# PSUM pools that take over banks wait for single tiles; transposes spread three steps apart: a routed attention with a feed-forward on one core

## Chip, core and metric

The kernel runs on one core of a Trainium2 chip. The metric is the device time of one execution in microseconds (us), lower is better. A core has five engines with queues of their own: TensorE (PE, with its weight loads as PEld), VectorE (DVE), ScalarE (ACT), GpSimd (POOL) and SyncE (SP), which issues transfers. Each executes its instructions in program order and waits at semaphores for the others.

## What is computed

Attention for 4 batches of 8 heads, 768 positions, head size 64. A query sees only those keys that are nearest to the same one of 16 centroids of its head. The result goes through a normalization and a gated feed-forward from 512 to 1536 and back.

```python
q_assign = np.argmax(np.einsum('bhsd,hcd->bhsc', q_n, c_n), axis=-1)
k_assign = np.argmax(np.einsum('bhsd,hcd->bhsc', k_n, c_n), axis=-1)
mask = q_assign[:, :, :, None] == k_assign[:, :, None, :]
scores = scale * np.matmul(q, k.transpose(0, 1, 3, 2))
scores = np.where(mask, scores, -1000000000.0)
scores = scores - np.max(scores, axis=-1, keepdims=True)
attn = np.exp(scores)
attn = attn / (np.sum(attn, axis=-1, keepdims=True) + 1e-09)
out = np.matmul(attn, v)
# ... heads side by side: x is [3072, 512]
rms = np.sqrt(np.mean(x * x, axis=-1, keepdims=True) + 1e-06)
xn = x / rms * rms_g
g = xn @ w_gate
silu = g * (1.0 / (1.0 + np.exp(-g)))
val = xn @ w_val
return silu * val @ w_out
```

## The kernel before

Work goes by pairs of heads (16 pairs `pi`) and by steps: 9 score chunks for each of the 32 heads ("slots"). Pair `pi` has its scores in steps `18 pi` to `18 pi + 17`. The main loop issues a step's scores, a piece of the feed-forward, the product with the values for the head before, and then whatever was put at that step with `at(step, fn)`. The order of the calls is the order of the instructions on each engine.

The preparation of a pair has thirteen parts. Four transposes on PE (T0 to T3, tile `tp`), each copied to SBUF; the casts into `aug` on GpSimd (CAST); the centroid products (SP, tile `sp`); then on VectorE a chain that makes the one-hot rows: transpose to `tr`, maximum `mx`, comparison `oh`, its scaling, transpose back to `ohT` (TR, MX, CMP, SCL, BACK); four transfers of `ohT` into `aug` (PLACE); and the cast of the values (CASTV).

```python
        def t_group(g):
            # ...
                tp = t_tile("tp")              # one bank of ps_t in the main loop
            for i in range(TH):
                nc.tensor.transpose(tp[:, i * P:(i + 1) * P], src[:, a, i * P:(i + 1) * P], ident_f)
            # ...
            if on_dve:
                nc.vector.tensor_copy(dst, tp)
            else:
                nc.scalar.copy(dst, tp)
```

Up to step 95 (`FFN0 = 96`) a score tile `scw` is three banks wide and serves three steps; there are two of them. From step 96 on the same six banks are given to `sc` (two), `gv` (two), `d` and `t` (one each), and the feed-forward runs beside the attention.

```python
    def score_chunk(slot, j):
        # ...
        if slot * NCH + j < FFN0:
            if j % WCH:
                return
            nch = WCH                          # 3
            sc = late["wide"].tile([P, WCH * CH], F32, name="scw", tag="scw")
        else:
            sc = late["sc"].tile([P, CH], F32, name="sc", tag="sc")
        # ... matmuls of aug with aug
        nc.scalar.activation(pts[slot][:, j * CH:(j + nch) * CH], sc[:, :nch * CH], ACT.Exp, scale=scale)
```

The product with the values goes into `acc`, of which there is one tile (`ps_pv`, `bufs=1`): six groups, in chunks 2 to 7 of the next head; in chunk 8 `pv_norm` divides it into `x`, after which the next head may use it.

```python
    def pv_norm(slot):
        # ...
        nc.vector.reciprocal(inv, acc[:, :, D:D + 1])
        nc.vector.tensor_tensor(x_t[b][:, :, h * D:(h + 1) * D], acc[:, :, 0:D],
                                inv.to_broadcast([P, ST, D]), op=ALU.mult)
```

At the end of a batch `x` is squared and summed by position block (`sumsq`, tiles `jk` and `ss`; for batch 0 first the columns of six heads, then those of the last two), raised to -1/2 on GpSimd (`ir`), scaled to `xn` and turned by PE (`turn`, tile `tx`) or by a transfer into `xnT`, the operand of the feed-forward (`gp`, `vp`, `dp`).

```python
    first.close()
    late["wide"] = wide.enter_context(tc.tile_pool(name="ps_wide", bufs=2, space=PSUM))
    # ...
    for step in range(NT):
        slot, j = divmod(step, NCH)
        if step == FFN0:
            wide.close()
            for nm, bufs in (("sc", 2), ("gv", 2), ("d", 1), ("t", 1)):
                late[nm] = ctx.enter_context(tc.tile_pool(name="ps_" + nm + "2", bufs=bufs, space=PSUM))
        score_chunk(slot, j)
        ffn_next(min(B, max(0, (step - LAG) // (H * NCH))) * 2 * FC, on_act=False)
        flush(1)
        if slot > 0 and 2 <= j < 2 + ST:
            pv_group(slot - 1, j - 2)
        if slot > 0 and j == 2 + ST:
            pv_norm(slot - 1)
        extras(step)
```

Of the kernel before, what the change touches and what calls it, by code (L numbers as in the profile page):

```python
# [13 lines left out]
PSUM = bass.MemoryType.PSUM  # L14
# [5 lines left out]
def kernel(  # L20
# [12 lines left out]
    nc = tc.nc  # L33
    B, H, S, D = q.shape
    NC = centroids.shape[1]
    DM, DF = moe_w_gate.shape
# [31 lines left out]
    wide = ExitStack()  # L68
    WCH = 3
    late = {}  # L70
# [16 lines left out]
    def load_pair(pi, kinds=range(3)):  # L87
        for kind in kinds:
            load_part(pi, kind)
# [7 lines left out]
    g_b = const.tile([P, DM], F32, name="g_b")  # L97
# [64 lines left out]
    def w_load(i):  # L162
        if i < 8:
            j, kind = divmod(i, 2)
            c = slice(j * DF // 4, (j + 1) * DF // 4)
            nc.gpsimd.dma_start(out=(wg, wv)[kind][:, :, c],
                                in_=(moe_w_gate, moe_w_val)[kind][:, c].rearrange("(c p) f -> p c f", p=P))
        else:
            j = i - 8
            nc.gpsimd.dma_start(  # L170
                out=wo[:, 3 * j:3 * j + 3, :],
                in_=moe_w_out[j * 3 * P:(j + 1) * 3 * P, :].rearrange("(c p) d -> p c d", p=P))
# [114 lines left out]
    def score_chunk(slot, j):  # L287
        pi, a = divmod(slot, 2)
        ag = aug[pi % NSET][a]
        if j == 0:  # L290
            pts[slot] = ptp.tile([P, ST * S], BF16, name="pT", tag="pT")
        nch = 1
# [3 lines that stand above are left out]
            nch = WCH  # L296
# [3 lines that stand above are left out]
        lo = j * CH  # L300
        while lo < (j + nch) * CH:
            kc, qo = divmod(lo, S)
            o = lo - j * CH
            n = min(CH - o % CH, S - qo)
            nc.tensor.matmul(sc[:, o:o + n], lhsT=ag[:, 1, kc * P:(kc + 1) * P],  # L305
                             rhs=ag[:, 0, qo:qo + n], start=True, stop=True)
            lo += n
        nc.scalar.activation(pts[slot][:, j * CH:(j + nch) * CH], sc[:, :nch * CH], ACT.Exp, scale=scale)  # L308
# [3 lines left out]
    def pv_group(slot, g):  # L312
        pi, a = divmod(slot, 2)
        vb = vbf[pi % NSET]
        if g == 0:
            accs[slot] = ps_pv.tile([P, ST, D + 1], F32, name="acc", tag="acc")
        acc = accs[slot]
        for kc in range(ST):
            nc.tensor.matmul(acc[:, TORD[g], :], lhsT=pts[slot][:, kc * S + g * P:kc * S + (g + 1) * P],  # L319
                             rhs=vb[:, a, TORD[kc], :], start=(kc == 0), stop=(kc == ST - 1))  # L320

    def pv_norm(slot):
        b, h = divmod(slot, H)
        if h == 0:
            x_t[b] = xp.tile([P, ST, DM], BF16, name="x", tag="x")
        acc = accs.pop(slot)
        inv = small.tile([P, ST, 1], F32, name="inv", tag="inv")
# [3 lines that stand above are left out]
# [121 lines left out]
    def flush(keep=0):  # L452
        while len(pend) > keep:
            pend.pop(0)()
# [4 lines left out]
    def ffn_next(limit, tail=False, on_act=True):  # L459
        n, kind = divmod(fpos[0], 3)  # L460
        if n >= limit:
            return False
        fpos[0] += 1
        ffn_piece(n, kind, tail, on_act)
        return True
# [6 lines left out]
    def at(step, fn):  # L472
        extra.setdefault(step, []).append(fn)

    T0, T1, T2, T3, CAST, SP, TR, MX, CMP, SCL, BACK, PLACE, CASTV = range(13)
# [22 lines left out]
    p1[CAST]()  # L498
    keep_warm(9, w_ps)
    first.close()  # L500
    late["wide"] = wide.enter_context(tc.tile_pool(name="ps_wide", bufs=2, space=PSUM))
    for i, step in ((SP, 0), (TR, 1), (MX, 1), (CMP, 2), (SCL, 2), (BACK, 3), (PLACE, 3), (CASTV, 3)):
        at(step, p1[i])
    at(3, lambda: load_part(2, 2))
    at(5, lambda: load_part(3, 2))
    at(8, lambda: load_pair(4))
    for i, step in ((CAST, 4), (SP, 6), (TR, 7), (MX, 9), (CMP, 10), (SCL, 10), (BACK, 12), (PLACE, 12), (CASTV, 13)):
        at(step, p2[i])
    at(22, lambda: load_pair(5))
    at(30, lambda: nc.sync.dma_start(out=g_b, in_=moe_rms_g.unsqueeze(0).to_broadcast([P, DM])))  # L510

    at(49, lambda: nc.gpsimd.tensor_scalar_mul(g_b, g_b, DM ** 0.5))
    for b in range(B):
        sumsq, inv, norm, turn = rms_parts(b)
        if b == 0:
            plan = [(sumsq, (-9, 0, 2), (0, 1, 2), 0), (sumsq, (8, 8, 8), (0, 1, 2), 1), (inv, (8,), (0,), 2),
                    (norm, (12, 17, 18), (0, 1, 2)), (turn, (17, 20, 22), (0, 1, 2)),
                    (sumsq, (27, 29, 30), (3, 4, 5)), (inv, (30,), (1,)), (norm, (32, 33, 34), (3, 4, 5))]
        else:
            plan = [(sumsq, (9, 9, 10), (0, 1, 2)), (inv, (11,), (0,)), (norm, (12, 13, 15), (0, 1, 2)),  # L520
                    (sumsq, (19, 19, 25), (3, 4, 5)), (inv, (26,), (1,)), (norm, (27, 28, 29), (3, 4, 5))]
        for fn, steps, items, *more in plan:
            for step, it in zip(steps, items):
                at(H * NCH * (b + 1) + step, lambda fn=fn, it=it, more=more: fn(it, *more))
    for pi in range(3, B * NP):
        base = 2 * NCH * (pi - 2) + {7: 17, 8: 6}.get(pi, 0)
        steps = (-8, -6, -4, -2, 0, 1, 3, 4, 5, 6, 7, 8, 10)
        if pi == 3:
            steps = (-9, -7, -5, -3, 0, 1, 3, 4, 5, 6, 7, 8, 10)
        elif pi == 6:  # L530
            steps = (-8, -6, -4, -2, 0, 1, 3, 4, 5, 5, 6, 7, 21)
        elif pi > 6:
            steps = (-5, -4, -3, -2, 0, 1, 2, 3, 4, 5, 6, 6, 10)
        for fn, step in zip(prep_parts(pi), steps):
            at(base + step, fn)
        if pi < B * NP - 3:
            at({6: 100, 7: 118}.get(pi, base + 12), lambda pi=pi: load_pair(pi + 3))
    for i, step in enumerate((44, 50, 57, 65, 72, 78, 95, 100, 105, 111, 117, 123)):
        at(step, lambda i=i: w_load(i))
    def extras(step):  # L540
        for fn in extra.get(step, ()):
            fn()

    for step in range(NT):
        slot, j = divmod(step, NCH)
        if step == FFN0:
            wide.close()
            for nm, bufs in (("sc", 2), ("gv", 2), ("d", 1), ("t", 1)):
                late[nm] = ctx.enter_context(tc.tile_pool(name="ps_" + nm + "2", bufs=bufs, space=PSUM))
        score_chunk(slot, j)  # L550
        ffn_next(min(B, max(0, (step - LAG) // (H * NCH))) * 2 * FC, on_act=False)
        flush(1)
# [5 lines that stand above are left out]
# [41 lines left out]
```

## Time and profile before

| what | value |
|---|---|
| time, median of 3 | 354.16 us (353.92 to 356.08) |
| span of the profiled execution | 352.4 us |
| mean granted clock of TensorE | 0.995 of full |
| busy: PE, ACT, DVE, POOL | 337.2, 226.6, 223.9, 89.0 us |
| transferred | 34.98 MB, mean 99 GB/s |

The page gives each engine's busy time, the costliest groups of instructions and the chain of work that ended last. In a line of waits "A <- B: total, times, longest" says how long engine and instruction A stood idle until B released it. A line of the timeline has start, length, engine, source line, operation, output and inputs, shapes and count; in brackets the idle time before it and its releaser. Matmuls are pipelined and their ends are modelled, so the distance between starts says more than the length. A granted clock below 1.00 makes each matmul longer without showing idle time.

### The profile page before, as it was taken

What the parts mean: (1) busy time and instruction counts of PE and PEld (TensorE: products, weight loads), DVE (VectorE), ACT (ScalarE), POOL (GpSimd) and SP (SyncE); (2) the same over time, 40 slices, a digit from 0 to 9 for tenths busy, and PEclk for the clock granted to TensorE, in tenths of its full rate; (3) what the DMA queues carried; (4) which work ended last, traced back from release to release, by engine and by line L of the source; (5) the groups of instructions that cost most, each with busy time, mean ns of one, the idle gap of its engine ahead of it and who ended that gap; (6) DMA issues with size and microseconds to landing.
All of it is one profiled execution on the core that took longest, in us unless ns stands there. A gap on an engine that the chain in (4) does not pass through costs nothing.

```text
span 352.4 us, 7515 instructions
## 1 busy us (share of the span) xinstructions
PE 337.2 (96%) x2960; PEld 205.1 (58%) x2960; DVE 223.9 (64%) x460; ACT 226.6 (64%) x389; POOL 89.0 (25%) x123
## 2 busy tenths in 40 slices
PE   8988998899999999999999999999999998999996
PEld 3556665566656566665656566556666654555543
DVE  4786678588774678757566567765554686655540
ACT  3688888787767687766667677777777253323322
POOL 2676854256520324211030304020000011000000
PEclk9999999899999999999999999999999999999999
DMA  7766999947784007161411002220000021300012
GB/s 233 231 210 197 214 250 232 225 59 109 160 222 148 30 15 207 43 168 42 129 50 42 32 12 56 55 53 32 30 8 27 30 56 52 76 30 30 32 60 89
DMA packets 36770, 34.98 MB, mean 99 GB/s; under 512 B 13520, under 2 KB 33664, under 8 KB 36736
## 3 DMA queue, kind: packets, MB, share of 16 engines
q1 hardware_dynamic: 30240, 29.20, 26.6%
q0 software_dynamic: 5984, 4.84, 9.8%
q10 hardware_dynamic: 512, 0.48, 0.5%
q8 instruction: 23, 0.38, 0.4%
q14 instruction: 11, 0.09, 0.1%
HBM read 28.61 MB, written 6.29 MB: 99 GB/s over the span
## 4 chain that ended last, share of the span: by engine, by line
PE 81%; DVE 10%; ACT 3%; DMA 2%; issue 2%; POOL 1%; SPq 0%; DVEq 0%; ACTq 0%; POOLq 0%
PE dp L440 17%; PE gp L407 17%; PE vp L407 16%; PE sc L305 11%; PE acc L319 8%; PE tp L201 5%; PE scw L305 4%; PE sp L237 3%; DVE xn L373 2%; DVE qk L205 2%; DMA k_in<-in_k_dram 1%; ACT pT L308 1%; DVE oh L254 1%; DVE gvT L422 1%; DVE x L329 1%
## 5 line engine op out<-in xcount | busy, mean ns | idle before, releaser
L308 ACT ACTIVATE pT<-sc 128x512 bf16<-128x512 f32 x192 | 113.4, 597 | 47.4 <-PE sc L305 46.4
L416 DVE SCALAR_TENSOR_TENSOR uu<-th,gp 128x384 f32<-128x384 f32 x96 | 53.0, 552 | 62.1 <-ACT th L412 62.0
L407 PE MATMUL vp<-xnT,wv 128*128 128x384 bf16 x384 | 78.1, 325 | 1.8 <-DVE gvT L422 1.8
L407 PE MATMUL gp<-xnT,wg 128*128 128x384 bf16 x384 | 78.1, 325 | 0.5 <-DVE gvT L422 0.5
L440 PE MATMUL dp<-wo,gvT 128*128 128x512 bf16 (+1 forms) x300 | 76.1, 370 | 1.9 <-ACT ob L446 1.9
L412 ACT ACTIVATE th<-gp 128x384 f32<-128x384 f32 x96 | 47.2, 492 | 46.3 <-PE gp L407 43.3
L319 PEld LDWEIGHTS <-pT 128*128 128x128 bf16 x1152 | 57.9, 98 | 29.5 <-issue 3.9
L305 PE MATMUL sc<-aug 80*128 80x512 bf16 (+1 forms) x256 | 72.6, 326 | 1.2 <-ACT pT L308 1.2
L224 POOL CAST aug<-qk 64x768 bf16<-64x768 f32 x60 | 51.7, 862 | 57.5 <-DVE qk L205 50.0
L319 PE MATMUL acc<-vbf,pT 128*128 128x65 bf16 x1152 | 63.4, 194 | 2.1 <-DVE x L329 2.1
L407 PEld LDWEIGHTS <-wg 128*128 128x128 bf16 x384 | 37.1, 97 | 31.9 <-issue 1.3
L422 DVE TENSOR_TENSOR gvT<-uu,vp 128x384 bf16<-128x384 f32 x96 | 52.4, 546 | 4.9 <-PE vp L407 0.4
L308 ACT ACTIVATE pT<-scw 128x1536 bf16<-128x1536 f32 x32 | 44.9, 1452 | 10.3 <-PE scw L305 10.2
L407 PEld LDWEIGHTS <-wv 128*128 128x128 bf16 x384 | 37.0, 97 | 21.0 <-issue 2.7
L305 PEld LDWEIGHTS <-aug 80*128 80x128 bf16 x384 | 33.9, 98 | 19.5 <-issue 8.8
L440 PEld LDWEIGHTS <-gvT 128*128 128x128 bf16 x300 | 29.1, 98 | 26.9 <-issue 2.9
L205 DVE COPY qk<-tp 128x384 f32<-128x384 f32 x40 | 21.9, 554 | 25.9 <-PE tp L201 25.6
L305 PE MATMUL scw<-aug 80*128 80x512 bf16 (+1 forms) x128 | 27.0, 334 | 0.9 <-issue 0.7
L364 POOL TENSOR_SCALAR ir<-ss 128x3 f32<-128x3 f32 x7 | 1.7, 236 | 95.1 <-ACT jk L350 84.7
L373 DVE SCALAR_TENSOR_TENSOR xn<-x,ir,g_b 128x512 bf16<-128x512 bf16 x24 | 20.6, 871 | 6.9 <-POOL ir L365 5.8
L229 POOL CAST vbf<-v_in 128x768 bf16<-128x768 f32 x16 | 13.5, 845 | 38.5 <-issue 38.2
L329 DVE TENSOR_TENSOR x<-acc,inv 128x384 bf16<-128x384 f32 x32 | 17.8, 557 | 1.1
(62 smaller groups left out, 212.2 us busy)
## 6 DMA issues: line engine op xcount, KB each, us to landing
q_in<-in_q_dram SPq DMA_DIRECT2D x16, 384.0 KB, 5.3
k_in<-in_k_dram SPq DMA_DIRECT2D x16, 384.0 KB, 6.0
out_dram<-ob SPq DMA_DIRECT2D x23, 256.0 KB, 2.0
v_in<-in_v_dram SPq DMA_DIRECT2D x15, 384.0 KB, 6.2
wg<-in_moe_w_gate_dram POOLq DMA_DIRECT2D x4, 384.0 KB, 6.3
wv<-in_moe_w_val_dram POOLq DMA_DIRECT2D x4, 384.0 KB, 7.4
wo<-in_moe_w_out_dram POOLq DMA_DIRECT2D x4, 384.0 KB, 6.2
aug<-ohT SPq DMA_DIRECT2D x57, 24.0 KB, 1.9
```

What stands on the lines that cost most here:

```text
L205: nc.vector.tensor_copy(dst, tp)
L224: nc.gpsimd.tensor_copy(aug[st][a][0:D, :, par * HS:(par + 1) * HS], qk32[0][par * D:(par + 1) * D, 2 * a:2 * a + 2, :])
L305: nc.tensor.matmul(sc[:, o:o + n], lhsT=ag[:, 1, kc * P:(kc + 1) * P], rhs=ag[:, 0, qo:qo + n], start=True, stop=True)
L308: nc.scalar.activation(pts[slot][:, j * CH:(j + nch) * CH], sc[:, :nch * CH], ACT.Exp, scale=scale)
L319: nc.tensor.matmul(acc[:, TORD[g], :], lhsT=pts[slot][:, kc * S + g * P:kc * S + (g + 1) * P], rhs=vb[:, a, TORD[kc], :], start=(kc == 0), ...
L329: nc.vector.tensor_tensor(x_t[b][:, :, h * D:(h + 1) * D], acc[:, :, 0:D], inv.to_broadcast([P, ST, D]), op=ALU.mult)
L373: nc.vector.scalar_tensor_tensor(st["xn"][:, tl, :], x_t[b][:, t, :], st["ir", m][:, tl:tl + 1], g_b, op0=ALU.mult, op1=ALU.mult)
L407: nc.tensor.matmul(pt[:, :HS], lhsT=w[:, dc, fc * P:(fc + 1) * P], rhs=xnT[b, m][:, :, dc, :], start=(dc == 0), stop=(dc == DC - 1))
L412: nc.scalar.activation(th, pt[:, :HS], ACT.Tanh, scale=0.5)
L416: nc.vector.scalar_tensor_tensor(uu, th, 1.0, pt[:, :HS], op0=ALU.add, op1=ALU.mult)
L422: nc.vector.tensor_tensor(gvT[half][:, fc, :], uu, pt[:, :HS], op=ALU.mult)
L440: nc.tensor.matmul(dp, lhsT=gvT[hf][:, f, tl * P:(tl + 1) * P], rhs=wo[:, f, cols], start=(f == 0), stop=(f == FC - 1))
```

## The change

Two things are meant. The pools that take over PSUM banks from a closed pool get `reuse_waits="tile"`: a new tile then waits for the old tiles that lay in its banks, not for the whole pool before. And the steps at which preparation is issued move: the transposes of pairs 3 to 6 are spread (three steps apart for 4 to 6), the one-hot chain is moved by a step here and there, the squares at the end of batch 0 are put between the transposes of pair 6 (steps 63, 65 and 68 for 63, 72 and 74), the scaling of `g_b` and most of the weight loads come earlier, and the cast of the values of pair 6 moves from step 93 to 79.

```diff
-    late["wide"] = wide.enter_context(tc.tile_pool(name="ps_wide", bufs=2, space=PSUM))
+    late["wide"] = wide.enter_context(tc.tile_pool(name="ps_wide", bufs=2, space=PSUM,
+                                                 reuse_waits="tile"))
...
-    for i, step in ((CAST, 4), (SP, 6), (TR, 7), (MX, 9), (CMP, 10), (SCL, 10), (BACK, 12), (PLACE, 12), (CASTV, 13)):
+    for i, step in ((CAST, 4), (SP, 6), (TR, 7), (MX, 8), (CMP, 10), (SCL, 11), (BACK, 13), (PLACE, 13), (CASTV, 14)):
         at(step, p2[i])
...
-    at(49, lambda: nc.gpsimd.tensor_scalar_mul(g_b, g_b, DM ** 0.5))
+    at(46, lambda: nc.gpsimd.tensor_scalar_mul(g_b, g_b, DM ** 0.5))
...
-            plan = [(sumsq, (-9, 0, 2), (0, 1, 2), 0), (sumsq, (8, 8, 8), (0, 1, 2), 1), (inv, (8,), (0,), 2),
+            plan = [(sumsq, (-9, -7, -4), (0, 1, 2), 0), (sumsq, (8, 8, 8), (0, 1, 2), 1), (inv, (8,), (0,), 2),
...
-        steps = (-8, -6, -4, -2, 0, 1, 3, 4, 5, 6, 7, 8, 10)
+        steps = (-11, -8, -5, -2, 0, 0, 2, 3, 4, 5, 6, 7, 10)
         if pi == 3:
-            steps = (-9, -7, -5, -3, 0, 1, 3, 4, 5, 6, 7, 8, 10)
+            steps = (-9, -6, -4, -2, 0, 1, 3, 4, 5, 6, 7, 8, 10)
         elif pi == 6:
-            steps = (-8, -6, -4, -2, 0, 1, 3, 4, 5, 5, 6, 7, 21)
+            steps = (-11, -8, -5, -2, 0, 0, 2, 3, 4, 4, 5, 6, 7)
...
-    for i, step in enumerate((44, 50, 57, 65, 72, 78, 95, 100, 105, 111, 117, 123)):
+    for i, step in enumerate((44, 49, 54, 60, 66, 71, 75, 77, 105, 111, 117, 123)):
         at(step, lambda i=i: w_load(i))
...
-                late[nm] = ctx.enter_context(tc.tile_pool(name="ps_" + nm + "2", bufs=bufs, space=PSUM))
+                late[nm] = ctx.enter_context(tc.tile_pool(name="ps_" + nm + "2", bufs=bufs, space=PSUM,
+                                                          reuse_waits="tile"))
```

The thirteen numbers of `steps` are those of T0, T1, T2, T3, CAST, SP, TR, MX, CMP, SCL, BACK, PLACE and CASTV, counted from `base = 18 (pi - 2)`: a pair is prepared two pairs ahead of its scores.

## The prediction

> **What bounds the kernel now.** I read the page first, then the list of waits of TensorE, then busy time and clock in short stretches, then the timeline around the two longest waits.
>
> ```profile
> PE 337.2 (96%) x2960; PEld 205.1 (58%) x2960; DVE 223.9 (64%) x460; ACT 226.6 (64%) x389; POOL 89.0 (25%) x123
> ```
>
> PE leaves only 352.4 - 337.2 = 15.2 us idle, so no schedule change can win more than a few per cent. PE's named waits are few:
>
> ```profile
> PE acc L319 <- DVE x L329: 2.1, 2, 1.4
> PE dp L440 <- ACT ob L446: 1.9, 4, 0.7
> PE vp L407 <- DVE gvT L422: 1.8, 4, 0.5
> PE tp L201 <- DVE qk L205: 1.6, 5, 0.6
> PE sc L305 <- ACT pT L308: 1.2, 1, 1.2
> ```
>
> The dp and vp waits lie after 80 us, in work whose order the change leaves alone. The other three are in the wide stage: about 14.4 to 68.1 us, steps 0 to 95, attention without the feed-forward. The stretches there show more than the waits do (columns: PE, PEld, DVE, ACT, POOL busy, then granted clock, DMA share, GB/s):
>
> ```profile
> 58.00:59.00 1.00, 0.35 (x3) 0.00 (x0) 0.93 (x4) 1.00 (x2) 0.00 (x0) 1.00 0.89 155
> 59.00:60.00 1.00, 0.23 (x7) 0.26 (x8) 0.90 (x5) 0.97 (x1) 0.00 (x0) 1.00 1.22 180
> 60.50:61.00 0.50, 0.50 (x14) 0.39 (x12) 0.29 (x3) 0.20 (x1) 0.02 (x1) 0.90 1.31 203
> 61.00:61.50 0.50, 0.50 (x12) 0.50 (x10) 0.00 (x0) 0.50 (x1) 0.50 (x1) 0.50 1.33 207
> 64.00:64.50 0.50, 0.50 (x4) 0.30 (x3) 0.50 (x2) 0.50 (x2) 0.17 (x1) 0.69 0.94 350
> 67.00:68.00 1.00, 0.00 (x0) 0.00 (x0) 0.14 (x1) 1.00 (x1) 0.00 (x0) 1.00 1.07 201
> ```
>
> PE starves at 58 to 60 us; then its clock is half from about 60.9 to 64.3 us (0.90 and 0.69 in the edge stretches give the ends), and "busy" hides that. At 67 to 68 us it does nothing. The timeline tells why:
>
> ```profile
> 54.56 0.68 DVE L352 SCALAR_TENSOR_TENSOR jk<-x 128x384 bf16<-128x384 bf16 x1
> 55.29 1.05 DVE L352 SCALAR_TENSOR_TENSOR jk<-x 128x384 bf16<-128x384 bf16 x1
> 56.27 0.57 DVE L244 STREAM_TRANSPOSE tr<-sp 128x384 f32<-128x384 f32 x1
> 59.07 0.56 DVE L329 TENSOR_TENSOR x<-acc,inv 128x384 bf16<-128x384 f32 x1
> 59.77 0.34 PE L319 MATMUL acc<-vbf,pT 128*128 128x65 bf16 x6 [1.43 <-DVE x L329]
> ...
> 66.52 0.35 PE L319 MATMUL acc<-vbf,pT 128*128 128x65 bf16 x6
> 68.08 0.38 PE L305 MATMUL sc<-aug 80*128 80x512 bf16 x1 [1.22 <-ACT pT L308]
> ```
>
> Two squares of the batch end stand ahead of the one-hot chain (tr to ohT) on VectorE; that chain stands ahead of the normalization x, the only thing that frees the single acc tile. One pair earlier tr comes 0.92 us after its sp (44.67 to 45.59); here 54.00 to 56.27, 2.27.
>
> **What the Trainium skill says.** "TensorE: Matmul & The Clock Gate", Part 1 (The HAM clock gate): the array clock falls to half after a window of low activity of about 3.4 us and returns after a busy one. The length agrees (60.9 to 64.3). Its advice to avoid gaps above about 3 us is too lenient here: 1.43 us of named idle, in two microseconds that were 0.35 and 0.23 busy, was enough. "Advanced Engine Details and Errata", VectorE Performance Modes: VectorE's second SBUF port is shared with GpSimd and the two block each other. The trace agrees: the scaling L260 takes 0.25 us alone (38.09) and 0.72 under GpSimd casts (28.42); xn takes 0.74 alone and 1.29 under one (61.91). "Perfetto Trace Analysis", Per-instruction lifecycle: the time for a semaphore to arrive lies outside the reported windows; here exponentials end 0.3 us before the scores that need their tile.
>
> **The change part by part.** In the instruction order of the two built kernels the matmuls, exponentials and transfers are the same in number; only order and waits differ. Times below are starts read from the timeline, and a step costs the distance from its start to the next start on PE. A tensor's name stands for the instruction that writes it.
>
> *1. Transposes.* A steady pair of heads (18 steps) runs from one odd head's first scores to the next, 48.21 to 57.54 us: 9.33. PE does in it six score tiles, twelve acc groups, four transposes (T0 to T3) and one sp. Its bubbles: T2 comes 0.81 us after its 12 acc, which elsewhere take 0.36 (0.45 lost, one ps_t bank, copy by VectorE); sp 0.81 after scores that take 0.65 (0.16); the first scores of the odd head 0.71 after 12 acc (0.35, an exponential). Sum 0.96, leaving 8.37. With T0 moved ahead of those scores, T0 fills the 0.35, and T2 finds the copy of T1 done. But a transpose needs 1.17 us after the one before (50.26 to 51.43), and T0 to T1 is now only 0.36 + 0.65 = 1.01: 0.16 lost. And VectorE's order becomes copy of T0, then inv and x: the copy begins 0.56 after T0, lasts 0.56, inv and x 0.75, so acc goes on 1.95 us after T0 where PE is ready at 1.17 + 0.36 = 1.53: 0.42 lost. The 0.16 before sp stays. New bubbles 0.74, a pair about 9.1: 0.2 to 0.3 saved in each of two full pairs (18 to 36, 36 to 54), 0.1 in steps 9 to 18. Sum 0.6.
>
> *2. Last pair of the batch (54 to 72).* Same, but squares now stand between the copies. The first (0.68) lets T1's copy just in time; the next overlap casts and take 1.05, holding T2's copy and thus T3 and sp by about 0.5. Net loss 0.2.
>
> *3. Square out of the way.* No square ahead of tr: with sp at s, tr s + 0.92, chain 2.69 (45.59 to 48.28), inv and x to s + 4.3, acc at s + 4.4 instead of 5.77 (59.77 - 54.00). Then three squares of 0.34, ss, pow 0.9 and xn. In this trace x to tx took 3.68 us (59.63 to 63.31); xn at 0.74 instead of 1.29, with the vbf cast now earlier, gives 3.1: tx at s + 7.4, where it was 9.31, scores after it at 7.75 (were 9.72). With the full clock (no starving, so no half-clock window) the remaining scores, 18 acc and two tx take 2.95 us to the place of the first sc: s + 10.7; before, 66.52 + 0.19 = 66.71 is s + 12.71. Saved 2.0.
>
> *4. PSUM takeover.* sc and the first gp lie in banks of the older scw tile and need its exponential alone; vp needs the younger one's. In the trace PE could have gone on at 66.71 and went at 68.08. Now sc goes at once, gp follows the xnT copy, 0.3 us later (0.22 before), vp comes when its exponential is done. 1.37 - 0.1 = 1.3 saved. The same keyword at the opening saves nothing: those scores wait for the aug transfer.
>
> *5. g_b scale at 46.* It now stands ahead of the vbf cast in GpSimd's queue, so it runs right after a weight issue, about 37.5 to 39 us, on top of cmp and scaling of that pair. By the port sharing, 0.3 to 1.2 us more VectorE chain ahead of x, which then holds acc. Loss 0.6.
>
> *6. Weights earlier.* The place transfers land in 2.7 to 6.9 us, but are needed about 28 steps, 14 us, later. Nothing on the path.
>
> Sum: 0.6 - 0.2 + 2.0 + 1.3 - 0.6 = 3.1. After the switch PE is 99% busy (59.5 of 60 us) with unchanged order, so the gain is carried to the end: 354.16 - 3.1, about 351.
>
> **The rivals.** (a) *ScalarE takes over.* Six exponentials of 1.37 us are 8.22 per pair against PE's 8.37: nearly equal. For: ScalarE is busy 0.97 to 1.00 in each of 57 to 60 us. Against: its idle in a steady pair is 0.69 + 0.28. It caps part 1 and delays sc behind an exponential; then the total gain is near 2 us: 352. (b) *VectorE as gate:* squares and g_b slide into the copies; every acc waits for x, and a second half-clock window may follow. For: the 1.05 and 1.29 us outliers. Then only the switch is kept: 353 or a little above 354. (c) *Everything meets:* no port contention, pairs near 8.5 us; 0.8 in two pairs, 3.3 in parts 3 and 4 and no g_b loss give 5: 349.
>
> **Range and chances.** The middle is 350.9; (c) sets the low end at 348.7, (b) the high end at 353.2. Over 2% needs below 347.1, 7 us, while the wide stage's 32 exponentials alone take 44.9 of its 53.7 us, so that nearly all of its slack would have to go: 0.04. Slower by 2% needs 361.2: two or three new stalls each with a half-clock window: 0.02. Within 2%: 0.94.
>
> **What would show it.** Right: first sc directly after the last acc, the wait on pT gone; clock 1.00 throughout 58 to 66 us; tr within 1 us of sp at the batch end; a T2 without wait; acc waiting about 0.4 us for x after T1 in each pair; L260 or L254 long once near 38 us. Wrong: scw waiting for ScalarE, a half-clock window elsewhere, or changes after 80 us beyond the shift.

## The result and the profile after

| what | before | after |
|---|---|---|
| time, median (range), 4 executions each | 354.36 us (353.92 to 356.08) | 350.61 us (350.48 to 350.84) |
| span of the profiled execution | 352.4 us | 348.5 us |
| mean granted clock of TensorE | 0.995 | 0.999 |
| ratio of times, 95% interval | | 0.9888 (0.9859 to 0.9917) |

The page of the changed kernel, busy time by engine:

```profile
PE 335.5 (96%) x2960; PEld 203.5 (58%) x2960; DVE 223.5 (64%) x460; ACT 226.1 (65%) x389; POOL 89.0 (26%) x123
```

The span fell by 3.9 us, PE's busy time by 1.7. So 2.2 us were idle time of PE, and the rest was time in which it ran slowly: the clock, which the next view shows. This divides PE's time, not the gain: what the full clock is worth is asked below. These are the stretches of the changed kernel around the batch end (columns as before: PE, PEld, DVE, ACT, POOL busy, clock, DMA share, GB/s):

```profile
56.00:58.00 2.00, 1.52 (x22) 0.81 (x19) 1.86 (x7) 2.00 (x3) 0.89 (x2) 1.00 1.18 280
58.00:60.00 2.00, 2.00 (x38) 1.59 (x36) 0.91 (x6) 2.00 (x2) 0.90 (x1) 1.00 1.16 296
60.00:62.00 2.00, 1.55 (x19) 1.01 (x16) 1.97 (x5) 2.00 (x4) 0.00 (x0) 1.00 1.32 231
62.00:64.00 2.00, 1.89 (x31) 1.49 (x31) 1.07 (x3) 2.00 (x3) 0.00 (x0) 1.00 1.27 224
```

The hole of 58 to 60 us (0.35 and 0.23 busy) has become two small ones, 0.48 us in 56 to 58 and 0.45 us in 60 to 62, and the clock stays full. TensorE's waits of the changed kernel, from the start to 70 us:

```profile
PE tp L201 <- DVE qk L205: 1.5, 2, 0.7
...
PE acc L319 <- DVE x L329: 0.5, 2, 0.3
...
PE tx L383 <- DVE xn L373: 0.3, 1, 0.3
PE tx L383 <- ACT xnT L385: 0.2, 1, 0.2
```

The wait of `acc` for `x` went from 2.1 to 0.5 us, the wait of `sc` for an exponential is gone. The transposes' 1.5 us are still there, but in two waits: 0.74 us at a T2 at 22.41 us and 0.73 us at a T1 at 30.07, where the copy of T0 stood behind a one-hot chain that GpSimd's casts had lengthened (L260 took 0.73 us there). From step 18 on no T2 waits. The same events in the timeline of the changed kernel at the batch end:

```profile
52.93 0.85 PE L237 MATMUL sp<-qk,cbd 128*32 128x384 f32 x8
53.85 0.58 DVE L244 STREAM_TRANSPOSE tr<-sp 128x384 f32<-128x384 f32 x1 [0.28 <-PE sp L237]
55.32 0.75 POOL L166 DMA_DIRECT2D wv<-in_moe_w_val_dram  x1
55.68 0.47 DVE L260 TENSOR_SCALAR oh<-oh 64x384 bf16<-64x384 bf16 x1
56.88 0.56 DVE L329 TENSOR_TENSOR x<-acc,inv 128x384 bf16<-128x384 f32 x1
57.58 0.34 PE L319 MATMUL acc<-vbf,pT 128*128 128x65 bf16 x6 [0.31 <-DVE x L329]
59.65 0.75 DVE L373 SCALAR_TENSOR_TENSOR xn<-x,ir,g_b 128x512 bf16<-128x512 bf16 x1 [1.02 <-POOL ir L361]
60.46 0.40 PE L383 MATMUL tx<-ident_b,xn 128*128 128x128 bf16 x4 [0.32 <-DVE xn L373]
63.57 0.35 PE L319 MATMUL acc<-vbf,pT 128*128 128x65 bf16 x6
63.76 0.38 PE L305 MATMUL sc<-aug 80*128 80x512 bf16 x1
```

`tr` stands 0.92 us after `sp`, no square between; `acc` goes on 4.65 us after `sp` (5.77 before), although L260 takes 0.47 us beside the issue of a weight load on GpSimd, for 0.25 before; the first `sc` follows the last `acc` at once.

Four starts on PE cut both kernels, and all runs below, into stretches: the first `scw`, the `sp` of the last pair (s), the first `tx`, the first `gp`.

| stretch, us | before | after | less by |
|---|---|---|---|
| first scw to s | 39.59 | 38.61 | 0.98 |
| s to first tx | 9.31 | 7.53 | 1.78 |
| first tx to first gp | 4.99 | 3.79 | 1.20 |
| first gp to end | 284.10 | 284.25 | -0.15 |

All of the gain lies before 65 us; the other 80% of the kernel are only shifted.

### The profile page after: what moved, and what is told of

It is laid out like the page before. It is cut to its first block, busy times and chain, and to the rows that moved or that the text cites. A ratio compares the mean times of both kernels' runs of the same rounds, so it can differ in the third digit from the quotient of the medians.

```text
span 348.5 us, 7510 instructions
## 1 busy us (share of the span) xinstructions
PE 335.5 (96%) x2960; PEld 203.5 (58%) x2960; DVE 223.5 (64%) x460; ACT 226.1 (65%) x389; POOL 89.0 (26%) x123
## 4 chain that ended last, share of the span: by engine, by line
PE 80%; DVE 9%; ACT 4%; DMA 3%; issue 2%; POOL 1%; SPq 0%; DVEq 0%; POOLq 0%; ACTq 0%
PE dp L440 17%; PE gp L407 17%; PE vp L407 16%; PE sc L305 11%; PE acc L319 8%; PE tp L201 5%; PE sp L237 3%; PE scw L305 3%; ACT pT L308 2%; DMA aug<-ohT 2%; DVE xn L373 2%; DVE qk L205 1%; DMA xnT<-xn 1%; PE w_ps L129 1%; DVE x L329 1%
## 5 line engine op out<-in xcount | busy, mean ns | idle before, releaser
L319 PEld LDWEIGHTS <-pT 128*128 128x128 bf16 x1152 | 57.0, 97 | 28.5 <-issue 2.5
L422 DVE TENSOR_TENSOR gvT<-uu,vp 128x384 bf16<-128x384 f32 x96 | 52.3, 545 | 4.9 <-PE vp L407 0.4
L305 PE MATMUL scw<-aug 80*128 80x512 bf16 (+1 forms) x128 | 26.1, 325 | 0.4 <-DMA aug<-ohT 0.2
```

Of the source, the lines that this page charges most:

```text
L422: nc.vector.tensor_tensor(gvT[half][:, fc, :], uu, pt[:, :HS], op=ALU.mult)
```

## The experiments

Two theories stood against each other. The first is the sum of the prediction: each part acts where it stands, the squares and the takeover carry most, and `g_b` costs something. The second is that the clock does it: PE starves at 58 to 60 us, that halves its clock, and whatever ends the starving or the half clock brings the gain. Ratios are against the kernel before, executed on the same chip.

**The three parts alone, on the kernel before.** e1 takes only the pools:

```diff
-    late["wide"] = wide.enter_context(tc.tile_pool(name="ps_wide", bufs=2, space=PSUM))
+    late["wide"] = wide.enter_context(tc.tile_pool(name="ps_wide", bufs=2, space=PSUM, reuse_waits="tile"))
...                                    (and the same keyword on the pools of step 96)
```

> The kernel before with the single-tile waits of the PSUM pools alone, all steps as before. Theory A (three separate waits were removed and their gains add up): the idle 1.22 us ahead of the first sc goes, the first gp starts 1.1 us sooner after the last acc, and the time falls by 1.0 to 1.3 us. Theory B (ScalarE is nearly full there, so the next exponential takes over as the limit): 0 to 0.3 us, and a wait of sc or vp for an exponential stands in its place.

353.40 us, ratio 0.9978 (0.9964 to 0.9991): 0.8 us less, between the two forecasts. In the trace the last `tx` to the first `gp` took 0.90 us, as in the changed kernel, for 2.01 before: the takeover is worth 1.1 us where it acts, and no wait for ScalarE stands in its place. Some 0.2 of it are lost after `gp` (284.27 us to the end for 284.10). At the opening the keyword brought nothing: the first `scw` still waits for the `aug` transfer (0.5 us), and the `sp` of step 18 stands at 25.30 us for 25.27. The waits of `acc` for `x` are untouched. TensorE's waits of e1, 14 to 70 us:

```profile
PE acc L319 <- DVE x L329: 2.1, 2, 1.4
...
PE tx L383 <- DVE xn L373: 0.9, 1, 0.9
```

The second line is new: the profiled execution of e1 had the full clock throughout, and there PE arrives early at `tx` and waits 0.9 us. Keep it in mind for the clock.

e2 takes only the squares:

```diff
-            plan = [(sumsq, (-9, 0, 2), (0, 1, 2), 0), ...
+            plan = [(sumsq, (-9, -7, -4), (0, 1, 2), 0), ...
```

> The kernel before with the three squares of batch 0 at steps 63, 65 and 68, nothing else. Theory A (the squares ahead of the one-hot chain hold acc, and the chain from x over ss, ir and xn to tx sets what follows): acc waits for x at most 0.4 us instead of 1.43, the clock stays at 1.00 from 58 to 66 us, xn still takes about 1.3 us because the cast of the values still lies over it; time lower by 0.8 to 1.4 us. Theory C (the half-clock window is the larger part of the loss): lower by 2 us or more.

352.72 us, ratio 0.9964 (0.9951 to 0.9977): 1.5 us less. s to the first `tx` went from 9.31 to 8.15 us: 1.16 us of it come from the squares' new place; the first `tx` to the first `gp` fell by another 0.46 with the clock at full. First `scw` to s stayed at 39.50, so the squares between the copies cost nothing even with the old steps.

e3 takes only the steps of the preparation (all tuples, the first pair's list and the earlier cast of the values):

```diff
-        steps = (-8, -6, -4, -2, 0, 1, 3, 4, 5, 6, 7, 8, 10)
+        steps = (-11, -8, -5, -2, 0, 0, 2, 3, 4, 5, 6, 7, 10)
...                                    (pairs 2, 3 and 6 likewise)
```

> The kernel before with the new steps of the pairs' parts alone (transposes three steps apart, cast of the values of pair 6 at step 79); squares, g_b, weight loads and PSUM waits as before. Theory A: the pairs from 18 to 72 gain about 0.9 us in all; the two squares still stand ahead of tr, so acc still waits over 1 us, and xn falls to about 0.75 us: time lower by 0.9 to 1.6 us. Theory B (ScalarE or VectorE takes over between the transposes): 0 to 0.4 us.

354.28 us, ratio 0.9997 (0.9978 to 1.0015): nothing in the median, although its trace shows the faster pairs (first `scw` to s 38.66 us for 39.59). That is the number of theory B, but nothing took over between the transposes; neither theory foresaw what follows. Timeline of e3:

```profile
57.41 0.73 DVE L260 TENSOR_SCALAR oh<-oh 64x384 bf16<-64x384 bf16 x1
...
58.87 0.56 DVE L329 TENSOR_TENSOR x<-acc,inv 128x384 bf16<-128x384 f32 x1
59.58 0.34 PE L319 MATMUL acc<-vbf,pT 128*128 128x65 bf16 x6 [1.81 <-DVE x L329]
61.65 0.75 DVE L373 SCALAR_TENSOR_TENSOR xn<-x,ir,g_b 128x512 bf16<-128x512 bf16 x1 [1.02 <-POOL ir L361]
```

Stretches of e3 there:

```profile
58.00:60.00 2.00, 0.42 (x8) 0.33 (x9) 1.86 (x7) 1.31 (x1) 0.04 (x1) 1.00 1.25 177
60.00:62.00 2.00, 2.00 (x28) 1.39 (x27) 0.91 (x6) 1.39 (x1) 1.28 (x2) 0.82 1.23 205
62.00:64.00 2.00, 2.00 (x21) 1.60 (x20) 1.55 (x4) 1.90 (x3) 1.14 (x2) 0.50 0.53 113
```

`acc` waits 1.81 us for 1.43 before: the two squares still stand ahead of the one-hot chain, and the earlier cast of the values, which now runs beside L260, makes that 0.73 us for 0.25. So `x` comes 5.54 us after `sp` (58.87 - 53.33), before it was 5.07 (59.07 - 54.00). Then the clock is half, and here that counts: `xn` is ready early (0.75 us long, its rival cast on GpSimd gone), so PE is the late one: the first `tx` to the first `gp` takes 5.38 us for 4.99. Of the 14 executions of e3 five had a mean clock of about 0.990, five of about 0.995 and four the full clock; those four have a median of 353.06 us, where the kernel before at full clock, on the same chip, has 354.07. So the steps bring 1.0 us, and the lost clock takes it back.

**The clock.** e4 leaves all steps as they were and only keeps PE busy in the hole, with six matmuls of zeros:

```diff
+    at(82, lambda: keep_warm(6, ps_t.tile([P, CH], F32, name="w_ps", tag="t")))
```

> The kernel before with six matmuls of zeros (128x512, into a spare tile of the transposes' bank, read by nobody) put where PE starves at the batch end: they fill the idle time and delay nothing. The clock should then stay at 1.00 from 58 to 66 us while every wait stays. Theory A (the chain from x to xn sets when PE can go on, so half speed cost nothing): the time stays within 0.3 us. Theory C (the half clock cost up to half of its 3.4 us): 0.7 to 1.7 us lower.

353.79 us, ratio 0.9985 (0.9972 to 0.9999), clock 0.998 or more in all 13 executions: 0.4 us less. How much of it is the clock is not settled. In the traces s to the first `gp` went from 14.30 to 13.78 us, 0.5 less; but those executions of the kernel before that had the full clock anyway (19 of the 35 beside this run) have a median of 354.07 us, only 0.1 below all 35. Either way it is below theory C's 0.7 to 1.7. TensorE's waits of e4, 14 to 70 us, say why so little:

```profile
PE sc L305 <- ACT pT L308: 1.1, 1, 1.1
PE tx L383 <- DVE xn L373: 0.9, 1, 0.9
...
PE acc L319 <- DVE x L329: 0.6, 1, 0.6
```

PE runs faster after the hole and then waits 0.9 us for `xn` and 1.1 for the exponential at the takeover (the 0.6 us of `acc` lie in an earlier pair, at 30.95 us). Before, the half clock lay on top of the first of these waits and hid it.

e9 joins e3 and e4 (the new steps and the six matmuls, the rest as before), to see whether the half clock is what ate the steps' gain:

```diff
+    at(82, lambda: keep_warm(6, ps_t.tile([P, CH], F32, name="w_ps", tag="t")))
-        steps = (-8, -6, -4, -2, 0, 1, 3, 4, 5, 6, 7, 8, 10)
+        steps = (-11, -8, -5, -2, 0, 0, 2, 3, 4, 5, 6, 7, 10)
...                                    (and the other edits of e3)
```

> The new steps alone (as in e3_steps_only) with the six matmuls of zeros of e4_warm_gap in the place where PE starves. Theory D (the new steps are worth about 1 us, but xn then no longer hides a half-clock window, and that window falls into most executions because acc still starves PE): every execution has a mean clock of 0.998 or more, the spread of over 2 us goes, and the time is 0.8 to 1.3 us below the kernel before. Rival (the steps alone are worth nothing, ScalarE or VectorE takes over): within 0.3 us of e4_warm_gap, 353.5 to 354.1.

352.98 us, ratio 0.9955 (0.9938 to 0.9971), the clock full in all six executions. With the clock held, the medians differ by 1.34 us from before; e4's matmuls alone made 0.40, which leaves the steps about 0.9. This agrees with the 1.0 us of e3's executions at full clock.

e11 is e3 once more, for another trace of it:

> The kernel of e3_steps_only once more, for one trace. Its executions had a mean clock of 1.000, 0.995 or 0.990. At 1.000 theory D expects no half-clock stretch between 58 and 68 us and a first gp about 1 us sooner after the first tx than with one such stretch (5.38 us with one); at 0.990 two windows of 3.4 us at half clock, and a time near 355.3 us.

353.93 us in one execution, so no ratio; it had a mean clock of 0.995, so that what was expected at 1.000 and 0.990 was not seen. Stretches of e11:

```profile
58.00:60.00 2.00, 0.81 (x10) 0.60 (x11) 1.86 (x9) 0.91 (x1) 0.00 (x0) 1.00 1.25 189
60.00:62.00 2.00, 2.00 (x23) 1.41 (x22) 0.95 (x4) 1.45 (x1) 1.67 (x2) 0.56 1.16 201
62.00:64.00 2.00, 2.00 (x21) 1.55 (x20) 0.98 (x4) 1.66 (x2) 0.77 (x2) 0.59 0.70 180
```

The same hole, the same fall. The lost clock, 2 x 0.44 + 2 x 0.41 = 1.7 us, is half of 3.4 us.

**Single terms, on the kernel after.** e5 puts the cast of the last pair's values back to step 93:

```diff
-            steps = (-11, -8, -5, -2, 0, 0, 2, 3, 4, 4, 5, 6, 7)
+            steps = (-11, -8, -5, -2, 0, 0, 2, 3, 4, 4, 5, 6, 21)
```

> The kernel after, with only the cast of the values of pair 6 put back to step 93. Theory A (VectorE and GpSimd block each other, and xn is on the path): the cast lies over the first xn again, which takes about 1.3 us instead of 0.75; tx and all after it come 0.5 us later, time 0.4 to 0.6 us above the kernel after. Rival (xn is hidden behind the scores and the products): the same within 0.2 us.

351.21 us (350.91 to 351.59), ratio 0.9914 (0.9895 to 0.9934), 0.6 above the changed kernel, and as much above e6 (350.37 to 350.72), which was measured beside it. s to the first `tx` is 8.15 us again for 7.53; TensorE waits for `xn`, and the timeline of e5 shows what lies beside it:

```profile
PE tx L383 <- DVE xn L373: 0.9, 1, 0.9
...
59.95 0.82 POOL L229 CAST vbf<-v_in 128x768 bf16<-128x768 f32 x1
60.02 1.30 DVE L373 SCALAR_TENSOR_TENSOR xn<-x,ir,g_b 128x512 bf16<-128x512 bf16 x1 [1.08 <-POOL ir L361]
```

Beside the cast on GpSimd `xn` takes 1.30 us, without it 0.75; taken away from there, 0.62 us are saved. So the earlier cast is the second half of step 3. The Trainium skill says in "Advanced Engine Details and Errata", VectorE Performance Modes, that VectorE's second SBUF port is shared with GpSimd and that the two block each other there; the two lengths agree with it, the port itself no trace shows.

e6 lets `g_b` land earlier, so that its scaling really starts at step 46:

```diff
-    at(30, lambda: nc.sync.dma_start(out=g_b, in_=moe_rms_g.unsqueeze(0).to_broadcast([P, DM])))
+    at(21, lambda: nc.sync.dma_start(out=g_b, in_=moe_rms_g.unsqueeze(0).to_broadcast([P, DM])))
```

> The kernel after, with only the transfer of g_b issued at step 21 instead of 30, so that its scaling on GpSimd does not wait for it and begins about 37.2 us instead of 38.09. This is the collision that the prediction counted with 0.6 us and that did not come. Theory A (it did not come only because the transfer was late): L260 of that pair takes 0.7 to 1.5 us instead of 0.25, acc of that pair waits that much longer, time 0.3 to 1.2 us above the kernel after. Rival (the chain has slack there): the same within 0.2 us.

350.59 us, ratio 0.9896 (0.9877 to 0.9914), no different from the changed kernel. In the timeline of the changed kernel the scaling comes after the one-hot rows:

```profile
37.46 0.25 DVE L260 TENSOR_SCALAR oh<-oh 64x384 bf16<-64x384 bf16 x1
...
38.09 1.52 POOL L513 TENSOR_SCALAR g_b<-g_b 128x512 f32<-128x512 f32 x1 [0.93 <-DMA g_b<-in_moe_rms_g_dram]
38.55 0.56 DVE L205 COPY qk<-tp 128x384 f32<-128x384 f32 x1 [0.22 <-PE tp L201]
```

and in that of e6 on top of them:

```profile
36.95 1.52 POOL L513 TENSOR_SCALAR g_b<-g_b 128x512 f32<-128x512 f32 x1
37.18 0.52 DVE L260 TENSOR_SCALAR oh<-oh 64x384 bf16<-64x384 bf16 x1
...
38.26 0.56 DVE L205 COPY qk<-tp 128x384 f32<-128x384 f32 x1
```

Without the 0.93 us wait the collision happens: L260 takes 0.52 us for 0.25. But the copy of T0, next on VectorE, begins 0.63 us after T0 in both (37.92 to 38.55 in the changed kernel, 37.63 to 38.26 in e6): VectorE had been waiting for PE there (0.22 us in the changed kernel), and the longer L260 only fills that slack. A steady pair is 9.08 us in both.

e7 loads the weights at the old steps:

```diff
-    for i, step in enumerate((44, 49, 54, 60, 66, 71, 75, 77, 105, 111, 117, 123)):
+    for i, step in enumerate((44, 50, 57, 65, 72, 78, 95, 100, 105, 111, 117, 123)):
```

> The kernel after, with only the weight loads at their old steps. Theory A (transfers are off the path, as predicted): the same within 0.2 us. Rival (the earlier loads keep GpSimd or the transfer engines free later): 0.3 us or more slower than the kernel after.

350.83 us, ratio 0.9904 (0.9885 to 0.9923), and every stretch within 0.1 us of the changed kernel's. Nothing on the path.

**What is left in a pair.** In the changed kernel PE waits twice in each pair. Timeline, pair 36 to 54:

```profile
37.92 0.52 PE L201 MATMUL tp<-ident_f,q_in 128*128 128x128 f32 x3
...
39.16 0.31 PEld L201 LDWEIGHTS tp<-ident_f,k_in 128*128 128x128 f32 x3 [0.46 <-DVE qk L205]
39.24 0.56 DVE L329 TENSOR_TENSOR x<-acc,inv 128x384 bf16<-128x384 f32 x1
...
39.86 0.36 PE L319 MATMUL acc<-vbf,pT 128*128 128x65 bf16 x6 [0.15 <-DVE x L329]
```

T1 waits for the copy of T0, and `acc` for `x`, which stands behind that copy on VectorE. e8 and e10 move the steps so that no copy and no late part of the chain stands there. e8 puts `x` ahead of the last part of the chain and `sp` later:

```diff
-        steps = (-11, -8, -5, -2, 0, 0, 2, 3, 4, 5, 6, 7, 10)
+        steps = (-10, -6, -3, 0, 1, 3, 4, 5, 9, 9, 10, 11, 10)
...                                    (pairs 3 and 6 likewise)
```

> A version meant to beat the kernel after: transposes of pairs 4 to 6 at -10, -6, -3 and 0, centroid products at +3, comparison, scaling and transpose back behind the normalization (steps 9, 9, 10), so that on VectorE x comes before the copy of T0 and before the second half of the one-hot chain. Theory A (in each pair PE loses about 0.24 us at T1, 0.33 at acc and 0.16 at sp, all to the order on VectorE): a full pair falls from 9.1 to 8.5 to 8.8 us and the time is 0.8 to 1.8 us below the kernel after. Theory B (ScalarE takes over as the limit at 8.3 to 9 us per pair): within 0.4 us of the kernel after, with scw waiting for exponentials.

350.83 us, ratio 0.9911 (0.9889 to 0.9933): nothing gained on the changed kernel. A steady pair fell from 9.08 to 8.99 us only. ScalarE in the timeline of e8:

```profile
37.31 8.34 ACT L308 ACTIVATE pT<-scw 128x1536 bf16<-128x1536 f32 x6 [0.65 <-PE scw L305]
...
46.29 5.57 ACT L308 ACTIVATE pT<-scw 128x1536 bf16<-128x1536 f32 x4 [0.64 <-PE scw L305]
```

Six exponentials now run back to back for 8.34 us, and 8.34 + 0.64 = 8.98 is the pair. The 0.64 us are a score tile that comes late: in this trace 2.09 us pass from one chunk of scores to the next (43.35 to 45.44), with `sp` and its `acc` groups between them. The wait has moved from PE to ScalarE. Theory B had this number, but with `scw` waiting for exponentials; it is the exponential that waits for `scw`.

e10 keeps `sp` at its place, puts T0 two steps earlier and `x` ahead of the chain's end:

```diff
-        steps = (-11, -8, -5, -2, 0, 0, 2, 3, 4, 5, 6, 7, 10)
+        steps = (-13, -8, -5, -3, 0, 0, 2, 3, 4, 8, 11, 12, 10)
         if pi == 3:
-            steps = (-9, -6, -4, -2, 0, 1, 3, 4, 5, 6, 7, 8, 10)
+            steps = (-9, -6, -4, -2, 0, 0, 2, 3, 4, 8, 11, 12, 10)
         elif pi == 6:
-            steps = (-11, -8, -5, -2, 0, 0, 2, 3, 4, 4, 5, 6, 7)
+            steps = (-13, -8, -5, -3, 0, 0, 2, 3, 4, 9, 9, 10, 7)
```

> Another version meant to beat the kernel after: transposes of pairs 4 to 6 at -13, -8, -5 and -3, the scaling and the transpose back of the one-hot chain behind the normalization (steps 8 and 11), so that x no longer stands behind them or behind a late copy of T0, and between two score tiles PE has nearly the same amount of other work. Theory A (PE's 0.24, 0.33 and 0.16 us per pair come from the order on VectorE alone): pairs of 8.4 to 8.7 us instead of 9.1, time 0.8 to 1.6 us below the kernel after. Theory B (ScalarE with 8.34 us per pair and only two score tiles cannot be kept fed): pairs of 8.9 or more, within 0.4 us of the kernel after.

348.98 us (348.60 to 349.84), ratio 0.9848 (0.9829 to 0.9867): below both kernels. It and the changed kernel were each measured against before, not beside one another; their intervals overlap, and their ranges of times do not. Timeline of e10:

```profile
33.52 0.85 PE L237 MATMUL sp<-qk,cbd 128*32 128x384 f32 x8
35.36 8.44 ACT L308 ACTIVATE pT<-scw 128x1536 bf16<-128x1536 f32 x6 [0.22 <-PE scw L305]
42.19 0.85 PE L237 MATMUL sp<-qk,cbd 128*32 128x384 f32 x8
```

From `sp` to `sp` a pair takes 8.67 us. Six exponentials take 8.44 of it, and ScalarE then waits 0.22 us for a score tile: here ScalarE and PE are both nearly full. First `scw` to s is 36.68 us, 1.93 less than in the changed kernel. No wait of T1 or of `acc` for `x` remains in the steady pairs.

## Why the prediction held

The sum was 3.1 us and the time fell by 3.55 against the 354.16 it started from; the profiled executions, each from its first `scw`, differ by 3.81 (0.98 + 1.78 + 1.20 - 0.15). By its own steps:

| step | predicted | measured, in the traces |
|---|---|---|
| 1 transposes | 0.6 | 0.2 + 0.32 + 0.26 = 0.8 |
| 2 last pair with squares | -0.2 | 0.2 |
| 3 square out of the way | 2.0 | 1.9 |
| 4 PSUM takeover | 1.3 | 1.1, less 0.15 after gp |
| 5 g_b at 46 | -0.6 | 0 |
| 6 weights | 0 | 0 |

*Step 1* was right in kind: T2 without a wait, and in its place T1 waiting for the copy of T0 and `acc` waiting for `x`. The wait of `acc` was mis-sized: 0.42 estimated, 0.15 measured on PE. The three terms are the stretches from the first `scw` to the `sp` of step 18, and the pairs 18 to 36 (10.06 to 9.74 us) and 36 to 54 (9.34 to 9.08). In the first of them e3's trace shows 0.1, so the other 0.1 may be the start of the stretch, which varies with a transfer.

*Step 2* failed. A square was to take 1.05 us under the casts and hold back T2's copy, T3 and `sp`. It did take that long, but in another place. Timeline of the changed kernel:

```profile
50.34 0.08 DVE L352 DVE_READ_ACCUMULATOR jk<-x 128x1 f32 x1
50.72 0.56 DVE L205 COPY qk<-tp 128x384 f32<-128x384 f32 x1 [0.29 <-PE tp L201]
51.19 1.21 DVE L352 SCALAR_TENSOR_TENSOR jk<-x 128x384 bf16<-128x384 bf16 x1
51.71 0.52 PE L201 MATMUL tp<-ident_f,k_in 128*128 128x128 f32 x3
52.33 0.55 DVE L205 COPY qk<-tp 128x384 f32<-128x384 f32 x1
```

The second square was done before T2's copy was due (VectorE then waited 0.29 us for PE). The third took 1.21 us, but T3 started only at 51.71, so its copy could hardly have begun before 52.3. The last pair is 9.13 us for 9.33: it gained as the others did.

*Step 3*: `acc` at s + 4.65 for 4.4 (0.22 of the difference is L260, which was counted with 0.25 us and took 0.47), `tx` at s + 7.53 for 7.4, the scores after it at s + 7.76 for 7.75, the place of `sc` at s + 10.83 for 10.7. The runs split the 1.78 us up to `tx` into 1.16 for the squares (e2) and 0.62 for the cast that no longer lies under `xn` (e5). The full clock, which the step counted in, adds little by itself: e4 shows 0.46 us from `tx` to `gp`.

*Step 4*: the mechanism is shown by e1 alone. The 1.37 us wait at `sc` went, but `gp` then stood 0.49 us after `sc` where it had stood 0.22, a little more than the 0.1 set aside, which makes 1.1 for 1.3.

*Step 5* failed in two ways: the scaling did not come on top of L260, since it waited 0.93 us for its own transfer, and where e6 removed that wait, the 0.27 us went into VectorE's slack. The step took a longer chain on VectorE for a later `x`, without looking for idle time between them. The losses of steps 2 and 5 that did not come, 0.4 + 0.6 us, are more than the whole distance between 3.1 and 3.81. That the sum came so near is in part luck: they were partly cancelled by what steps 3 and 4 had too high.

*Step 6* holds for the time, but not because the loads touch nothing: at 46.55 us L260 takes 0.47 us beside a load, and with the old steps (e7, at 46.86) 0.25. The 0.22 us go into VectorE's slack, as those of `g_b` do.

Of the rivals, (a) is wrong for this change: the list of waits names no `scw` or `sc` that waits for ScalarE, and what PE loses in a pair it loses to VectorE. (One `scw` at the batch end, at 56.46 us, comes 0.3 us late, when an exponential has ended; but the `acc` after it waits for `x` anyway.) In e10 it comes near. (b) is in part what e3 does: `acc` waits 1.81 us for `x` at the batch end, and the half clock counts in full. With the squares out of the way (e2), or with six matmuls in the hole (e9), the half clock did not come. Taken at full clock the parts alone bring 0.8 (e1, eight of 13 executions, 353.26 us), 1.35 (e2) and 1.0 us (e3), 3.2 in sum; all together bring 3.75 (354.36 - 350.61). The rest is about the size of the 0.62 us of the earlier cast of the values, which acts once the squares are away (e5); with the squares in place s to the first `tx` fell by 0.12 us only (9.13 in e9, 9.25 in e4). No run adds the parts two by two. (c) was within reach, with other steps: e10's pair of 8.67 us is near its 8.5.

## What to carry to other kernels

Look first for what stands ahead of the single buffer that everybody needs (here two squares ahead of `x`). If a part tried alone brings nothing, compare executions of equal clock before dropping it: e3 showed 0 in the median and 1.0 us at full clock. Before charging a slower instruction to the path, look for idle time of its engine between it and the next consumer. When several engines are within a few per cent of each other, move a wait on paper through all of them: e8 took it from PE to ScalarE and won nothing, e10 took it out and won 1.6 us.

## What the runs showed of the hardware

The half clock comes by chance, and each time for the same length: about 60.9 to 64.3 us in the kernel before, 61.3 to 64.7 in e3, and 3.4 us in e11. Of 55 executions of the kernel before, measured beside the experiments, 28 had a mean clock of 0.998 or more (median 354.12 us), 18 about 0.995 (354.20) and 9 about 0.990 (355.79). A mean of 0.995 is about 1.8 us lost of 352 and fits one window of 3.4 us at half clock, which loses 1.7; 0.990 would be two. The same hole brings it in one execution and not in another: e1's trace has `acc` waiting 1.4 us and the full clock. The Trainium skill, "TensorE: Matmul & The Clock Gate", Part 1 (The HAM clock gate), gives about 3.4 us as the width of the window after which the clock changes; the three traces agree.

What a window costs depends on what lies beside it: in the kernel before 0.1 us by the executions (0.5 us from s to the first `gp` by the traces of it and of e4), where PE would have waited for `xn` anyway; 1.1 us each in e3, whose executions at 1.00, 0.995 and 0.990 have medians of 353.06, 354.20 and 355.25. In e2, e4, e9, the changed kernel and its variants no execution fell below 0.998: removing 1.4 us of starving, or filling it with six matmuls of zeros, was enough. Left open: of the kernel before only one execution was traced, so whether the window always lies at 61 to 64 us was not seen; and none at 0.990 was, so where its second window would lie, and why it costs the kernel before 1.6 us where the first costs 0.1, is not known.
